# Retention followed by a multiplicative FFN: start-up orders, unswapped heads in first chunks, and two row products moved by half a step

## The chip, the cores and the metric

The kernel runs on one core of a Trainium2 chip. The metric is the device time of one execution in microseconds. Five executions of the kernel before gave 188.74, 189.39, 189.68, 190.88 and 192.08 us; the median, 189.68 us, is the time that the prediction refers to. One further execution was profiled.

The engines are called PE (TensorE, matrix products), PEld (its weight loads), DVE (VectorE), ACT (ScalarE), POOL (GpSimd) and SP (SyncE, which here issues nearly all DMAs). Matrix products write to PSUM banks, which DVE and ACT empty. Every engine works through its own instructions in the order in which the program gives them, and engines wait for each other by semaphores.

## The reference

There are 4 batches, 8 heads, 768 positions and a head size of 64. Per head a 64 x 64 state decays by a factor and takes up one outer product per position; its product with the query is the output. All heads of a position, 512 numbers, then pass a feed-forward block of width 1024 without biases:

```python
gamma = 1.0 - 2.0 ** (-5.0 - np.arange(H, dtype=np.float32))
for t in range(S):
    state = gamma[None, :, None, None] * state + np.einsum('bhd,bhe->bhde', k[:, :, t], v[:, :, t])
    y[:, :, t] = scale * np.einsum('bhd,bhde->bhe', q[:, :, t], state)
# x = y with the heads side by side, 3072 rows of 512
h = (x @ w1) * (x @ w2) @ w3
out = h @ w_out
```

## The kernel before

**Tiling.** The recurrence is done by chunks of C = 128 positions, in two halves s of L = 64. One step m treats one chunk of two batches (index e): there are NCH = 6 chunks to a pair of batches and two pairs, so NSTEP = 12, and steps 0 and 6 are first chunks, with no state behind them. The 8 heads are NP = 4 pairs p with r = 0, 1. Decays are split into factors per row: v is multiplied by VS when it is cast to 16 bits, the outputs by YS when they leave PSUM, the state by GS from chunk to chunk.

**The parts of a step.** `k_transposes`/`k_dma` and `q_transposes`/`q_dma` bring kT and qT. `scores(m)` (L367) makes 32 products of 64 x 64 into psA, and its `am_back(r)` (L374, DVE) masks them into `am`. `intra(m)` (L395) multiplies `am` by v into two banks psY (s = 0, 1). `kv(m)` (L415) makes the outer products psK of each half; `kv_back(0)` (L432 in a first chunk, L434 otherwise, DVE) and `kv_back(1)` (L429 on DVE, then L430 on POOL, which multiplies by GS) turn them into the states `t`. `inter(m)` (L460) adds the product of queries and states to psY. `outputs_back(m, s)` (L474, DVE) multiplies psY by YS into `XT[m]`, the input of the feed-forward block. These products use quarters of the 128 x 128 array: 64 x 64 with row group and column group chosen by the halves of the operands.

**Swapped heads.** In psY, half s = 1 has the two heads of a pair swapped between partitions 0 to 63 and 64 to 127: `side(s, r)` is `half(r ^ s)`. `outputs_back` puts them back, so for s = 1 it takes two DVE instructions on 64 partitions, each from one half of the partitions to the other. For s = 0 it is one on 128.

**The feed-forward block** works on transposed data. w3 and w_out are multiplied first, at the start: w3 is loaded, cast by ACT (L208), transposed by PE (L235, L244), copied by DVE (L227) and multiplied by w_out (L256, L269) to W3O. Then, per step, `a_unit(f)` and `b_unit(f)` (L494) make a 128-row block f of x @ w1 and x @ w2, ACT copies the first out of PSUM (`pa`, L503), and DVE multiplies the two into HT (L509). `o_unit(e)` (L519) multiplies the eight blocks of HT by W3O for one batch, ACT scales the result (L523) and a DMA stores it. These are called the row products here: `ab(f)` is a pair of them, 8 matmuls of 256 columns; an `o_unit` is 8 of 512.

**PSUM.** The pool `ps_f` has four banks. psF, psO and, from step 4 on, psK take them as they become free: a bank that `kv` fills is free again when its `kv_back` has read it. psY has banks Y0 and Y1, psA banks X0 and X1.

**Order.** The order of every engine is the order of the program, which is written by hand (`manual_schedule`). Loads go out on SP in the order of the calls; 22 staging buffers hold them, and the program's first lines issue all loads up to chunk 4. From line 539 to 668 stand steps 0 and 1 and the beginning of step 2, with `busy` and `keep_busy` calls that multiply zeros on PE. Then come `step2()` and `step(3)` to `step(12)`. From step 5 on a step has this order on PE: `intra(m-1)`, `kv(m)`, `scores(m)`, `inter(m-1)`, the two `o_unit`s of chunk m-2, and the eight `ab` of chunk m-1. On DVE it has the three instructions of `outputs_back(m-1)`, the two of `kv_back`, the two of `am_back`, and eight products L509. The last line of the loop over f in `step` (L743 to L744) puts `ab(4)` to `ab(7)` of chunk m-1 at the end of step m.

**Places that the change touches:** `output_decays` (L185 to L192), called at L554; `side` (L381); `back` in `kv` (L422 to L435); `inter` (L460); `outputs_back` (L468 to L478); the start-up from L584 to L658; and `step`.

Of the kernel before, what the change touches and what calls it, by code (L numbers as in the profile page):

```python
# [9 lines left out]
FP = mybir.dt.float32  # L10
HP = mybir.dt.float16
AF = mybir.ActivationFunctionType
MULT = mybir.AluOpType.mult
# [5 lines left out]
def kernel(  # L19
# [11 lines left out]
    nc = tc.nc  # L31
# [27 lines left out]
    def half(x):  # L59
        return slice(x * L, (x + 1) * L)  # L60
# [91 lines left out]
    if_i = const.tile([128, 2, L], mybir.dt.int32, name="if_i")  # L152
    nc.gpsimd.iota(if_i[:, :, :], pattern=[[L, 2], [1, 2], [2, 32]], base=1, channel_multiplier=0)
    LGH = const.tile([128, H], FP, name="LGH")
    LGP = const.tile([128, 2, H], FP, name="LGP")
    for h in range(H):
        nc.gpsimd.memset(LGH[:, h : h + 1], -math.log(gam[h]))
    for h in range(H):
        for s in range(2):
            u = h // 2 * 2  # L160
            nc.gpsimd.memset(LGP[half((h + s) % 2), s, u : u + 2], math.log(gam[h]))


    keep = const.tile([128, L], FP, name="keep")
# [6 lines left out]
        )  # L171

    VS = const.tile([128, H], FP, name="VS")
    YS = const.tile([128, 2, H, L], FP, name="YS")
    GS = const.tile([128, NP, 128], FP, name="GS")
    vs_x = const.tile([128, H], FP, name="vs_x")
    nc.vector.tensor_tensor(vs_x[:, :], ip_i[:, :], LGH[:, :], MULT)
    if_f = const.tile([128, 2, L], FP, name="if_f")
# [1 line left out]
    nc.scalar.activation(VS[:, :], vs_x[:, :], AF.Exp)  # L180
    for h in range(H):
        p, r = h // 2, (h % 2) * 64
        nc.gpsimd.memset(GS[r : r + 64, p, :], gam[h] ** C)

    def output_decays():  # L185
        for s in range(2):
            x = att.tile([128, H, L], FP, tag="s32", name="s32")
            nc.vector.tensor_tensor(
                x[:, :, :], if_f[:, s, :].unsqueeze(1).broadcast_to((128, H, L)),
                LGP[:, s, :].unsqueeze(2).broadcast_to((128, H, L)), MULT,  # L190
            )
            nc.scalar.activation(YS[:, s, :, :], x[:, :, :], AF.Exp)  # L192

    mark_t = const.tile([1, 1], HP, name="mark")
    XT = {}
# [184 lines left out]

    def side(s, r):
        return half(r ^ s)

    def intra(m):
        am, v16 = AMs[m], v16s[m]
        psYs[m] = ps = [bank(f"Y{s}", [128, NP * 2, L], FP, "psY") for s in range(2)]
        last = None
        for e in range(2):  # L390
            for p in range(NP):
                for s in range(2):
                    for r in range(2):
                        c0 = p * 128 + r * 64
                        last = nc.tensor.matmul(  # L395
                            ps[s][side(s, r), p * 2 + e, :], lhsT=v16[half(s), e, c0 : c0 + 64],
                            rhs=am[half(s), r, p * 2 + e, :], start=(e == 0 and p == 0),
                            stop=(m % NCH == 0 and s == 0 and e == 1 and p == NP - 1),
                        )
        return last  # L400

    def kv(m, psf=False):
        k16, v16 = k16s[m], v16s[m]
        c = m % NCH
        n = 2 if c < NCH - 1 else 1
        if psf:
            ps = [ps_f.tile([128, NP * 2, L], FP, tag="psF", name="psK") for s in range(n)]
        else:
            ps = [bank(f"X{s}", [128, NP * 2, L], FP, "psK") for s in range(n)]
        for e in range(2):  # L410
            for p in range(NP):
                for s in range(len(ps)):
                    for r in range(2):
                        c0 = p * 128 + r * 64
                        nc.tensor.matmul(  # L415
                            ps[s][half(r), p * 2 + e, :], lhsT=k16[half(s), e, c0 : c0 + 64],
                            rhs=v16[half(s), e, c0 : c0 + 64], start=True, stop=True,
                        )
        if c == 0:
            Ts[m, 0] = None  # L420

        def back(s, eng=nc.gpsimd):  # L422
            if s >= len(ps):
                return
            t16 = att.tile([128, NP * 2 * L], HP, tag="t16", name="t16", bufs=4)
            kvs = ps[s][:, :, :].rearrange("p u x -> p (u x)")
            if s == 1:
                s32 = att.tile([128, NP * 2 * L], FP, tag="s32", name="s32")
                nc.vector.tensor_tensor(s32[:, :], kvs, Ts[m, 1][:, :], ADD)  # L429
                eng.tensor_tensor(t16[:, :], s32[:, :], GS[:, :, :].rearrange("p a x -> p (a x)"), MULT)  # L430
            elif Ts[m, 0] is None:
                nc.vector.tensor_copy(t16[:, :], kvs)  # L432
            else:
                nc.vector.tensor_tensor(t16[:, :], kvs, Ts[m, 0][:, :], ADD)  # L434
            Ts[(m, 1) if s == 0 else (m + 1, 0)] = t16  # L435

        return back
# [14 lines left out]
    def inter(m, behind=None):  # L452
        ps = psYs[m]
        t = [Ts[m, s] for s in range(2)]
        for e in range(2):
            for p in range(NP):
                u = p * 2 + e
                for r in range(2):
                    for s in (1,) if t[0] is None else (0, 1):
                        mm = nc.tensor.matmul(  # L460
                            ps[s][side(s, r), u, :], lhsT=t[s][half(r), u * L : (u + 1) * L],
                            rhs=queries(m, e, p, s, r), start=False, stop=(e == 1 and p == NP - 1),
                        )
                        if behind is not None:
                            wait_for(mm, behind)
                            behind = None

    def outputs_back(m, s):  # L468
        if m not in XT:
            XT[m] = xpool.tile([128, NP * 2, 2, L], HP, tag="xt", name="xt")  # L470
        order = "p u (t i) -> p u t i"
        for to in (slice(0, 128),) if s == 0 else (half(0), half(1)):
            fr = to if s == 0 else half(1 - to.start // L)
            nc.vector.tensor_tensor(  # L474
                XT[m][to, :, s, :].rearrange("p u (i t) -> p u t i", t=2),
                psYs[m][s][fr, :, :].rearrange(order, t=2),
                YS[fr, s, :, :].rearrange(order, t=2), MULT,
            )  # L478

    class Ffn:  # L480
# [207 lines left out]
    def step(m):  # L688

        kv_backs = []  # L690

        def keys():
            if 3 < m < NSTEP:
                kv_backs.append(kv(m, True))

        if m > 4:
            last = intra(m - 1)
            last = ended(last)
            keys()
            if m < NSTEP:  # L700
                am_back = scores(m)
            inter(m - 1, last)
        else:
            inter(m - 1)
            keys()
            am_back = scores(m)
        outputs_back(m - 1, 0)
        outputs_back(m - 1, 1)
        if m >= NSTEP:
            return  # L710
        for kv_back in kv_backs:
# [24 lines left out]
        ffn[m - 1].ab(2)  # L736
        ffn[m - 1].ab(3)
        if m == 3:
            kv_back(1)
        if m % 2 == 0:  # L740
            q_cast(m + 2, nc.gpsimd)
            q_cast(m + 3, nc.gpsimd)
        for f in range(4, 8):  # L743
            ffn[m - 1].ab(f)  # L744

    step2()
    for m in range(3, NSTEP):
        step(m)
# [38 lines left out]
```

## Time and profile before

| | us |
|---|---|
| median of five executions | 189.68 |
| profiled execution, device time | 190.95 |
| its span, first to last instruction | 189.24 |
| PE busy | 176.6 (93%) |
| PE weight loads busy | 125.0 (66%) |
| DVE busy | 107.9 (57%) |
| ACT busy | 87.1 (46%) |
| POOL busy | 55.7 (29%) |

The DMA queues moved 40.25 MB, 213 GB/s over the span. The profiled execution was one of the longer ones, 1.27 us over the median; durations are taken from it, and times are counted from its span's start. In lists of groups "line engine op out<-in" names the kernel's line, the engine, and the tiles. In the list of waits stand the engine and line that waited, whom it waited for, the total, how often, and the longest. "Issue" is time in which an engine waited for nothing that the profile shows. In the answer by stretches each engine has busy time and, in brackets, its number of instructions; behind them stand PE's granted clock (1.00 is full speed), the busy share of the DMA engines and GB/s.

PE's busy time by stretch: 7.61 us in the first 10 us, 8.64 from 10 to 20, 9.73 from 20 to 30, 6.96 from 30 to 40, 9.32 from 60 to 70, 8.71 from 130 to 140, and 9.9 to 10.0 in the others up to 170.

### The profile page before, as it was taken

What the parts mean: (1) busy time and instruction counts of PE and PEld (TensorE: products, weight loads), DVE (VectorE), ACT (ScalarE), POOL (GpSimd) and SP (SyncE); (2) the same over time, 40 slices, a digit from 0 to 9 for tenths busy, and PEclk for the clock granted to TensorE, in tenths of its full rate; (3) what the DMA queues carried; (4) which work ended last, traced back from release to release, by engine and by line L of the source; (5) the groups of instructions that cost most, each with busy time, mean ns of one, the idle gap of its engine ahead of it and who ended that gap; (6) DMA issues with size and microseconds to landing.
All of it is one profiled execution on the core that took longest, in us unless ns stands there. A gap on an engine that the chain in (4) does not pass through costs nothing.

```text
span 189.2 us, 6256 instructions
## 1 busy us (share of the span) xinstructions
PE 176.6 (93%) x2655; PEld 125.0 (66%) x2655; DVE 107.9 (57%) x199; ACT 87.1 (46%) x170; POOL 55.7 (29%) x93
## 2 busy tenths in 40 slices
PE   7797998589999899999999999999979999999993
PEld 2353565258877578587785877858658688684872
DVE  1227447736166945956748577485674774845330
ACT  3477844445575354342644416444154353332432
POOL 7200234606741642172400826008251060000000
PEclk9999999979999999999999999999999999999999
DMA  5999999999899999999999999999969960200203
GB/s 192 376 386 400 276 205 262 399 406 255 180 231 244 195 214 194 242 243 267 218 182 239 238 258 205 177 230 246 262 152 206 210 173 0 77 37 3 111 3 111
DMA packets 87339, 40.25 MB, mean 213 GB/s; under 512 B 67728, under 2 KB 82320, under 8 KB 87312
## 3 DMA queue, kind: packets, MB, share of 16 engines
q1 hardware_dynamic: 86880, 39.33, 89.0%
q8 instruction: 21, 0.34, 0.8%
q10 hardware_dynamic: 432, 0.52, 0.8%
q14 instruction: 6, 0.05, 0.1%
HBM read 29.36 MB, written 6.29 MB: 188 GB/s over the span
## 4 chain that ended last, share of the span: by engine, by line
PE 79%; DVE 6%; DMA 5%; ACT 4%; issue 2%; SPq 2%; ACTq 0%; DVEq 0%
PE psF L494 37%; PE psO L519 21%; DMA stg<-in_moe_w_dram 5%; PE psF L605 4%; PE psW L269 3%; PE psY L395 2%; PE psA L367 2%; DVE xt L474 2%; PE psY L460 2%; SPq L63 2%; PE psG L494 2%; ACT w3h L208 2%; PE psK L415 1%; DVE am L374 1%; PE psTq L314 1%
## 5 line engine op out<-in xcount | busy, mean ns | idle before, releaser
L494 PE MATMUL psF<-xt,w 128*128 128x256 f16 x672 | 75.9, 273 | 0.0
L494 PEld LDWEIGHTS <-w 128*128 128x128 f16 x704 | 68.4, 98 | 10.2
L509 DVE TENSOR_TENSOR ht<-pa,psF 128x256 f16<-128x256 f32 x88 | 36.6, 419 | 36.6 <-PE psF L494 27.9
L503 ACT COPY pa<-psF 128x256 f32<-128x256 f32 x80 | 29.7, 371 | 35.3 <-PE psF L494 35.3
L519 PE MATMUL psO<-w3o,ht 128*128 128x512 f16 (+2 forms) x200 | 43.9, 371 | 1.3 <-DVE xt L474 1.3
L519 PEld LDWEIGHTS <-ht 128*128 128x128 f16 x200 | 18.5, 98 | 21.1 <-issue 1.6
L474 DVE TENSOR_TENSOR xt<-psY,YS 64x512 f16<-64x512 f32 (+1 forms) x36 | 26.2, 727 | 7.5 <-PE psY L460 7.1
L523 ACT ACTIVATE osb<-psO 128x512 f32<-128x512 f32 (+2 forms) x25 | 14.5, 580 | 33.3 <-PE psO L519 30.4
L430 POOL TENSOR_TENSOR t<-s,GS 128x512 f16<-128x512 f32 x10 | 12.7, 1273 | 55.4 <-DVE s L429 55.4
L302 POOL TENSOR_TENSOR v<-stg,VS 128x512 f16<-128x512 f32 x23 | 23.6, 1043 | 10.6 <-DMA stg<-in_v_dram 8.6
L281 POOL CAST q<-stg 128x1024 f16<-128x1024 f32 x9 | 9.3, 1038 | 26.3 <-DMA stg<-in_q_dram 26.3
L374 DVE TENSOR_TENSOR am<-psA,keep 128x512 f16<-128x512 f32 x24 | 15.4, 681 | 2.8 <-PE psA L367 2.7
L227 DVE COPY w3t<-psW 128x1024 f16<-128x1024 f16 x8 | 5.5, 692 | 13.4 <-PE psW L235 10.5
L295 ACT CAST k<-stg 128x1024 f16<-128x1024 f32 (+1 forms) x12 | 10.8, 899 | 1.7 <-DMA stg<-in_k_dram 1.7
L208 ACT CAST w3h<-stg 128x1024 f16<-128x1024 f32 x8 | 8.1, 1042 | 5.5 <-DMA stg<-in_moe_w_dram 5.5
L605 PE MATMUL psF<-xt,w 128*128 128x256 f16 x64 | 9.3, 302 | 0.1
L395 PE MATMUL psY<-am,v 64*64 64x64 f16 x384 | 6.2, 196 | 2.9 <-DVE xt L474 1.3
L395 PEld LDWEIGHTS <-v 64*64 64x64 f16 x384 | 4.4, 108 | 6.2 <-issue 5.8
L434 DVE TENSOR_TENSOR t<-psK,t 128x512 f16<-128x512 f32 x10 | 6.9, 690 | 2.6 <-PE psK L415 2.2
L537 PE MATMUL psZ<-zeros 128*128 128x512 f16 x16 | 6.9, 586 | 1.3 <-DVE zeros L144 1.3
L269 PE MATMUL psW<-wo,w3t 128*128 128x512 f16 x32 | 8.1, 380 | 0.0
L256 PE MATMUL psW<-wo,w3t 128*128 128x512 f16 x32 | 8.0, 384 | 0.0
(65 smaller groups left out, 128.0 us busy)
## 6 DMA issues: line engine op xcount, KB each, us to landing
stg<-in_moe_w_dram SPq DMA_DIRECT2D x16, 512.0 KB, 9.4
stg<-in_q_dram SPq DMA_DIRECT2D x12, 512.0 KB, 6.4
stg<-in_k_dram SPq DMA_DIRECT2D x24, 256.0 KB, 5.6
stg<-in_v_dram SPq DMA_DIRECT2D x24, 256.0 KB, 5.7
out_dram<-osb SPq DMA_DIRECT2D x22, 256.0 KB, 3.4
stg<-in_moe_w_out_dram SPq DMA_DIRECT2D x4, 512.0 KB, 7.8
out_dram<-osb ACTq DMA_DIRECT2D x1, 256.0 KB, 2.1
out_dram<-osb ACTq DMA_DIRECT2D x1, 160.0 KB, 1.8
```

Of the source, the lines that this page charges most:

```text
L269: nc.tensor.matmul(ps[:, :], lhsT=t[:, g * 128 : (g + 1) * 128], rhs=WO[g // 2][:, g % 2, :], start=(g == 0), stop=(g == 7),)
L302: eng.tensor_tensor(v16[:, e, :].rearrange("j (h d) -> j h d", d=D), v32[:, e, :].rearrange("j (h d) -> j h d", d=D), VS[:, :].unsqueeze(2 ...
L374: nc.vector.tensor_tensor(am[:, r, :, :], ps[r][:, :, :], keep[:, :].unsqueeze(1).broadcast_to((128, NP * 2, L)), MULT,)
L395: last = nc.tensor.matmul(ps[s][side(s, r), p * 2 + e, :], lhsT=v16[half(s), e, c0 : c0 + 64], rhs=am[half(s), r, p * 2 + e, :], start=(e ...
L430: eng.tensor_tensor(t16[:, :], s32[:, :], GS[:, :, :].rearrange("p a x -> p (a x)"), MULT)
L474: nc.vector.tensor_tensor(XT[m][to, :, s, :].rearrange("p u (i t) -> p u t i", t=2), psYs[m][s][fr, :, :].rearrange(order, t=2), YS[fr, s, ...
L494: nc.tensor.matmul(ps[:, :], lhsT=W[d][:, f * 128 : (f + 1) * 128], rhs=self.x(d), start=(d == 0), stop=(d == 3),)
L503: nc.scalar.copy(self.pa[f][:, :], ps[:, :])
L509: nc.vector.tensor_tensor(self.HT[:, f, :], self.pa.pop(f)[:, :], ps[:, :], MULT)
L519: nc.tensor.matmul(psO[:, :], lhsT=self.HT[:, f, e * 128 : (e + 1) * 128], rhs=W3O[f][:, cs], start=(f == 0), stop=(f == 7),)
L523: nc.scalar.activation(osb[:, cs], psO[:, :], AF.Copy, scale=final_scale)
L605: nc.tensor.matmul(ps[f // 2][:, f % 2, :], lhsT=W[d][:, f * 128 : (f + 1) * 128], rhs=f0.x(d), start=(d == 0 and f % 2 == 0), stop=(d == ...
```

## The change

There are seven edits.

1. YS holds one factor per pair of heads and position in place of one per (pair, batch): three variants, (s = 0), (s = 1, heads in place) and (s = 1, heads swapped). `output_decays` makes them in three DVE products of 128 x 256 and one Exp of 768 columns, and is called behind the first cast of w3 instead of behind the last cast of w_out. `outputs_back` reads YS with a stride of zero over the two batches.
2. GS shrinks to one number per pair and partition; POOL's product L430 reads it with a stride of zero.
3. In first chunks (steps 0 and 6) the heads of half s = 1 are not swapped, and `outputs_back(m, 1)` is one DVE instruction there.
4. In first chunks the copy of psK to `t` (L432) goes from DVE to ACT.
5. In step 0 `inter(0)` is called behind `outputs_back(0, 0)`, `v_cast(1)` and `kv_back(1)` of chunk 0, and `outputs_back(0, 1)` right behind it, ahead of `scores(1)` and its `am_back`s. PE's own order stays as it was.
6. In step 1 POOL casts W2[0] and W2[1] ahead of the state's product with GS, which moves behind `q_cast(2)`; its DVE sum stays between `by_rows(W1, ps, 1)` and `by_rows(W1, ps, 2)`.
7. In step 8 `ab(6)` and `ab(7)` of chunk 7 fall out; step 9, the tenth, has them behind `am_back` and ahead of `o_unit(0)` of chunk 7.

```diff
-    LGP = const.tile([128, 2, H], FP, name="LGP")
+    LGP = const.tile([128, 2, NP], FP, name="LGP")
...
-            u = h // 2 * 2
-            nc.gpsimd.memset(LGP[half((h + s) % 2), s, u : u + 2], math.log(gam[h]))
+            nc.gpsimd.memset(LGP[half((h + s) % 2), s, h // 2 : h // 2 + 1], math.log(gam[h]))
...
-    YS = const.tile([128, 2, H, L], FP, name="YS")
-    GS = const.tile([128, NP, 128], FP, name="GS")
+    YS = const.tile([128, 3, NP, L], FP, name="YS")
+    GS = const.tile([128, NP], FP, name="GS")
...
     def output_decays():
-        for s in range(2):
-            x = att.tile([128, H, L], FP, tag="s32", name="s32")
+        x = xpool.tile([128, 3, NP, L], FP, tag="xt", name="ys_x")
+        for n, (s, swap) in enumerate(((0, 0), (1, 0), (1, 1))):
             nc.vector.tensor_tensor(
-                x[:, :, :], if_f[:, s, :].unsqueeze(1).broadcast_to((128, H, L)),
-                LGP[:, s, :].unsqueeze(2).broadcast_to((128, H, L)), MULT,
+                x[:, n, :, :], if_f[:, s, :].unsqueeze(1).broadcast_to((128, NP, L)),
+                LGP[:, swap, :].unsqueeze(2).broadcast_to((128, NP, L)), MULT,
             )
-            nc.scalar.activation(YS[:, s, :, :], x[:, :, :], AF.Exp)
+        nc.scalar.activation(
+            YS[:, :, :, :].rearrange("p n a x -> p (n a x)"), x[:, :, :, :].rearrange("p n a x -> p (n a x)"), AF.Exp
+        )
...
-    def side(s, r):
-        return half(r ^ s)
+    def side(m, s, r):
+        return half(r if m % NCH == 0 else r ^ s)
...
-        def back(s, eng=nc.gpsimd):
+        def back(s, eng=nc.gpsimd, later=False):
...
-                eng.tensor_tensor(t16[:, :], s32[:, :], GS[:, :, :].rearrange("p a x -> p (a x)"), MULT)
+                def decay():
+                    eng.tensor_tensor(
+                        t16[:, :].rearrange("p (a x) -> p a x", a=NP), s32[:, :].rearrange("p (a x) -> p a x", a=NP),
+                        GS[:, :].unsqueeze(2).broadcast_to((128, NP, 2 * L)), MULT,
+                    )
+
+                if later:
+                    Ts[m + 1, 0] = t16
+                    return decay
+                decay()
             elif Ts[m, 0] is None:
-                nc.vector.tensor_copy(t16[:, :], kvs)
+                nc.scalar.copy(t16[:, :], kvs)
...
-        order = "p u (t i) -> p u t i"
-        for to in (slice(0, 128),) if s == 0 else (half(0), half(1)):
-            fr = to if s == 0 else half(1 - to.start // L)
+        swap = s == 1 and m % NCH > 0
+        for to in (half(0), half(1)) if swap else (slice(0, 128),):
+            fr = half(1 - to.start // L) if swap else to
+            n = fr.stop - fr.start
             nc.vector.tensor_tensor(
-                XT[m][to, :, s, :].rearrange("p u (i t) -> p u t i", t=2),
-                psYs[m][s][fr, :, :].rearrange(order, t=2),
-                YS[fr, s, :, :].rearrange(order, t=2), MULT,
+                XT[m][to, :, s, :].rearrange("p (a e) (i t) -> p a e t i", e=2, t=2),
+                psYs[m][s][fr, :, :].rearrange("p (a e) (t i) -> p a e t i", e=2, t=2),
+                YS[fr, s + swap, :, :].unsqueeze(2).broadcast_to((n, NP, 2, L))
+                .rearrange("p a e (t i) -> p a e t i", t=2),
+                MULT,
             )
...
     cast_w3(("c", 0), w3c_st[0])
+    output_decays()
     busy(8)
...
     cast_wo(3)
-    output_decays()
     cast_w3(4, w3_st[4])
...
     w3o_back()
-    inter(0)
     outputs_back(0, 0)
     v_cast(1, (nc.gpsimd, nc.gpsimd))
     backs[1](1)
+    inter(0)
+    outputs_back(0, 1)
     nc.gpsimd.tensor_copy(W1[1][:, :], w1_st[1][:, :])
...
     am_back(0)
     am_back(1)
-    outputs_back(0, 1)
     ps = four_banks()
...
     by_rows(W1, ps, 1)
-    kv_back(1)
     nc.gpsimd.tensor_copy(W2[0][:, :], w2_st[0][:, :])
     nc.gpsimd.tensor_copy(W2[1][:, :], w2_st[1][:, :])
+    decay = kv_back(1, later=True)
     by_rows(W1, ps, 2)
...
     q_cast(2, nc.gpsimd)
+    decay()
     by_rows(W2, ps, 2)
...
         am_back(0)
         am_back(1)
+        for f in behind.pop(m - 2, ()):
+            ffn[m - 2].ab(f)
         ffn[m - 2].o_unit(0)
...
         for f in range(4, 8):
-            ffn[m - 1].ab(f)
-
+            if f not in behind.get(m - 1, ()):
+                ffn[m - 1].ab(f)
+    behind = {7: (6, 7)}
     step2()
```

More of the change, by code (lines that the diff above doesn't have):

```diff
@@ L182 @@
         p, r = h // 2, (h % 2) * 64
-        nc.gpsimd.memset(GS[r : r + 64, p, :], gam[h] ** C)
+        nc.gpsimd.memset(GS[r : r + 64, p : p + 1], gam[h] ** C)
     def output_decays():
-        for s in range(2):
-            x = att.tile([128, H, L], FP, tag="s32", name="s32")
+        x = xpool.tile([128, 3, NP, L], FP, tag="xt", name="ys_x")
+        for n, (s, swap) in enumerate(((0, 0), (1, 0), (1, 1))):
             nc.vector.tensor_tensor(
-                x[:, :, :], if_f[:, s, :].unsqueeze(1).broadcast_to((128, H, L)),
-                LGP[:, s, :].unsqueeze(2).broadcast_to((128, H, L)), MULT,
-            )
-            nc.scalar.activation(YS[:, s, :, :], x[:, :, :], AF.Exp)
+                x[:, n, :, :], if_f[:, s, :].unsqueeze(1).broadcast_to((128, NP, L)),
+                LGP[:, swap, :].unsqueeze(2).broadcast_to((128, NP, L)), MULT,
+            )
+        nc.scalar.activation(
+            YS[:, :, :, :].rearrange("p n a x -> p (n a x)"), x[:, :, :, :].rearrange("p n a x -> p (n a x)"), AF.Exp
+        )
     mark_t = const.tile([1, 1], HP, name="mark")
@@ L395, in intra @@
                         last = nc.tensor.matmul(
-                            ps[s][side(s, r), p * 2 + e, :], lhsT=v16[half(s), e, c0 : c0 + 64],
+                            ps[s][side(m, s, r), p * 2 + e, :], lhsT=v16[half(s), e, c0 : c0 + 64],
                             rhs=am[half(s), r, p * 2 + e, :], start=(e == 0 and p == 0),
@@ L460, in inter @@
                         mm = nc.tensor.matmul(
-                            ps[s][side(s, r), u, :], lhsT=t[s][half(r), u * L : (u + 1) * L],
+                            ps[s][side(m, s, r), u, :], lhsT=t[s][half(r), u * L : (u + 1) * L],
                             rhs=queries(m, e, p, s, r), start=False, stop=(e == 1 and p == NP - 1),
```

## The prediction

> **What bounds the kernel now.** I read the chain that ended last first, then the waits of TensorE (PE), then timelines of every engine from 15 to 67 us and from 118 to 142 us, then busy time by stretches.
>
> The page's fourth part gives the chain's shares:
>
> ```profile
> PE 79%; DVE 6%; DMA 5%; ACT 4%; issue 2%; SPq 2%; ACTq 0%; DVEq 0%
> ```
>
> Behind 67 us nearly all of the chain is PE. A change there pays only where it closes a hole in PE's row. In front, the chain goes over loads, casts and VectorE (DVE). PE's waits, longest first, show the holes:
>
> ```profile
> PE psY L395 <- DVE xt L474: 1.3, 1, 1.3
> PE psO L519 <- DVE xt L474: 1.3, 1, 1.3
> ...
> PE psY L395 <- issue: 1.2, 1, 1.2
> ...
> PE psA L367 <- issue: 0.4, 1, 0.4
> ```
>
> The first and the third lie next to each other in the chain (start, length, what):
>
> ```profile
> 35.52 0.73 DVE xt L474
> 36.25 0.01 issue
> 36.26 0.73 DVE xt L474
> 36.99 0.04 issue
> 37.03 0.38 PE psY L395 x24
> 37.41 1.15 issue
> 38.57 0.25 PE psY L395 x6
> ```
>
> PE waits until the first chunk's two xt products are done, works for 0.38 us, and stands again in the middle of a matmul group, waiting for nothing that the profile names. The second wait is misnamed: `xt` had started at 135.40 and o_unit doesn't read it. I counted the matmuls ahead of each unexplained hole (the third number in brackets):
>
> ```profile
> 0.00:37.42 37.42, 31.51 (x351) 16.17 (x351) 18.07 (x30) 21.43 (x27) 12.10 (x51) 1.00 1.01 311
> 0.00:63.20 63.20, 55.77 (x735) 34.66 (x735) 31.04 (x55) 35.21 (x51) 21.06 (x61) 0.97 1.01 291
> 0.00:137.50 137.50, 129.11 (x2014) 89.49 (x2015) 80.84 (x147) 67.06 (x122) 49.10 (x87) 0.99 1.10 256
> ```
>
> 351, 735 and 2014 lie 384 and 1279 apart: 3 x 128 and, but for one, 10 x 128. With its weight load a matmul is two instructions, so the holes sit at the edges of blocks of 256 PE instructions. The page's DMA part agrees: queue q8, "instruction", brought 0.34 MB in 21 packets, 16 KB each, against 5310 matmuls and weight loads. In the trace's DMA records the packets in front of the holes ran at 36.24 to 37.19, 61.17 to 62.38 and 135.35 to 136.67; PE went on 1.4 to 1.6 us later. So a hole is a block of PE's program that came late. From PE's entry into the block ahead (matmuls 224, 608 and 1887, at 31.30, 59.29 and 134.06 us) to going on (38.57, 63.75, 138.23) it took 7.27, 4.46 and 4.17 us. Blocks full of 64x64 matmuls are run through faster than that.
>
> A last view, busy time by stretch (span, PE busy, ..., granted clock third from the end):
>
> ```profile
> 33.04:36.45 3.41, 2.48 (x41) 1.07 (x42) 2.90 (x6) 2.16 (x4) 2.82 (x3) 1.00 1.01 400
> 36.45:39.87 3.42, 1.69 (x68) 1.26 (x68) 1.22 (x2) 1.04 (x1) 0.44 (x1) 1.00 1.01 408
> 39.87:43.28 3.41, 3.41 (x47) 2.30 (x45) 1.67 (x4) 1.04 (x1) 0.00 (x0) 0.50 1.05 385
> 135.44:138.86 3.42, 2.13 (x10) 0.87 (x9) 3.33 (x5) 0.22 (x1) 1.01 (x1) 1.00 1.15 196
> ```
>
> After a stretch with PE busy for 1.69 us of 3.42 the clock was 0.50 for 3.41 us, which costs 3.41/2 = 1.7 us. After 2.48 and 2.13 us it stayed at 1.00.
>
> **The change, part by part.** (a) *YS early.* In before, DVE makes two `s` products at 16.02 (1.28 us) and ScalarE (ACT) two Exp at 16.74 (1.23 us), ahead of the cast of w3 rows 4 at 17.88, whose data landed at 16.2. Moved to the start, three products of 128x256 (under 0.64 us each, the 128x512 row) fall into DVE's idle 4.77 us before 7.06, and the Exp of 768 columns (0.62 x 1.5 = 0.93) into ACT's 2.12 us before 8.05: free. The casts then follow the landings (16.2, 17.5, 18.8, 20.1), PE reaches w3_mm(6) about 0.8 us sooner, and meets the next limit: k's second half lands at 26.37, its ACT cast (0.62) ends at 27.02, so the key transposes can end at 27.44 instead of 28.06. The first chunk's am and intra come 0.4 to 0.65 us sooner; I take 0.65.
>
> (b) *First chunk.* DVE loses the copy of psK (0.69, L432) and one of the two half products (0.73), and the other stands ahead of am(1). The copy goes to ACT (0.60 by the 128x512 row of L208) at about 31.2, when kv(0) ends; ACT's kT copies wait until 32.06, so it is covered, with 0.2 us to spare. DVE: xt half 0 at 31.0 to 31.73, s at 31.87 to 32.54, then inter(0) is ready and xt half 1 runs to 33.3; scores(1) end at 33.7, am(1) at 35.0. intra(1) can start at 35.05 instead of 37.03: 2.0 us sooner.
>
> (c) *What is late next* is matmul 352, 24 matmuls into intra(1), reached at 35.4. Its block is asked for 0.65 us sooner (30.65). With the 7.27 us of the same place it goes on at 37.92; with the 4.46 us of the next place it would be there at 35.1, before PE. The lower gain is 0 (transfer paced by the loads in front), the upper 38.57 - 35.4 = 3.2. The load is the same at that place, so I take 7.27: **gain 0.65 us**, not 2.0. PE's idle time there becomes 0.4 + 2.5 us, against 1.5 + 1.15 now, so I leave the halved clock in place: 0 (end of the range: 1.7 gained).
>
> (d) *GpSimd's (POOL) order and the late decay.* POOL idled 7.55 us before 44.44, waiting for `s`. Now the W2 casts go ahead; from 39 to 58 us PE has no wait for them in before, so this gives 0, and covers PE being sooner: W2[0] and W2[1] land at 41.16 and 42.44, casts done by 43.5, needed at about 46. The decay moves behind q_cast(2) (48.05 to 49.3); `t` is read by the next chunk's DVE add at 60.72. q_cast(3) and k_cast(2) behind it on POOL end by 51, needed at 53. GS with a stride of zero: L302 reads VS that way at 1.04 us, the decay has 1.27; either is hidden. The block at matmul 736 shifts with its entry: 0; if it came at its old time, the 0.65 would be lost.
>
> (e) *Sixth-chunk start.* DVE saves 0.73 + 0.69 us and ACT gets 0.60 in its 2.4 us wait for psO; PE has no hole from 75 to 135 us: 0. The new patterns of xt keep 512 elements: 0.73, as now. If they cost some tenths more, PE's cover is the free banks behind o_unit.
>
> (f) *Tenth step.* 16 matmuls (1.75 us) move behind inter(8) and in front of o_unit of chunk 7. The block in front of matmul 2015 then lasts 1.5 us longer (1.75 less the 24 intra matmuls that fall out), more than the 1.29 us that it was late: that hole closes. But HT 6 and 7 now come on DVE behind these:
>
> ```profile
> 135.40 2.20 DVE L474 TENSOR_TENSOR xt<-psY,YS 128x512 f16<-128x512 f32 x3 [0.81 <-PE psY L460]
> 137.64 0.69 DVE L434 TENSOR_TENSOR t<-psK,t 128x512 f16<-128x512 f32 x1
> 138.36 0.69 DVE L429 TENSOR_TENSOR s<-psK,t 128x512 f32<-128x512 f32 x1
> 138.97 1.28 DVE L374 TENSOR_TENSOR am<-psA,keep 128x512 f16<-128x512 f32 x2
> ```
>
> From the first to the last it is 140.25 - 135.40 = 4.85 us. inter(8) now ends 1.75 us sooner, so DVE starts at 133.65 and am ends at 138.5; the two ht products (0.42 each, 0.40 apart) end at 138.9 and 139.25. PE has run the 16 matmuls and six of o_unit(0) by then (the kv banks, held until L434 and L429 end at 136.6 and 137.3, already stop it for about 1 us), waits, ends o_unit(0) at 139.5 and o_unit(1) (8 x 0.2225) at 141.3. In before that end was 140.33: **loss 0.97 us**. The 1.29 us hole is exchanged for 2.4 us of waiting for DVE and banks. In an execution whose block is not late the loss is 2.3.
>
> **Sum** on the profiled execution: 190.95 - 0.65 + 0.97 = 191.27, of which the span is 189.24 + 0.32 and 1.7 lies around it. That execution is 1.27 above the median, so I carry the difference: 189.68 + 0.32 = 190.0.
>
> The Trainium skill speaks to two terms. "Runtime: NRT & Kernel Launch", section "Instruction fetch mechanics", says that each engine streams its program in 16 KiB blocks of 256 instructions while it runs the one before, and that crossing an edge is mostly hidden; the block size agrees with the counts, the hiding doesn't (1.15, 0.40 and 1.29 us of holes). Were it hidden, (c) would give 2 us and (f) cost 2.3. "TensorE: Matmul & The Clock Gate", Part 1, says that the clock is halved after an idle window of about 3.4 us; here it was halved with no wait over 1.5 us. By the page's rule the tenth step couldn't lose its clock and the slower rival below would go.
>
> **Rivals.** *Faster: the block is there in time.* At the 4.46 us of the second place, intra(1) runs through, 3.2 us are gained, the stretch stays busy and the clock whole (1.7 more): 189.68 - 3.2 - 1.7 + 0.97 = 185.8. Two thirds of the wait gone and the clock kept gives about 187.5. For it: two of three places took 4.2 to 4.5. Against: the loads of w1 and w2 are at their densest there (400 GB/s). Chance 0.2, at 187.
>
> *Slower: the clock is halved in the tenth step.* Its waits of 0.45, 0.7, 0.95 and 0.2 us lie between 135.0 and 139.3; a 3.41 us stretch from 135.9 holds 1.56 us of work, under the 1.69 that lost the clock; one from 134.5 holds 2.2, over the 2.13 that kept it. Somewhere between it decides, and how the stretches fall is chance. Price 1.7: 191.7; if the block also wasn't late in most executions of before, 193.0. Chance 0.3.
>
> *The change doesn't do what it says:* the block edge slips to another instruction of step nine and PE waits for both. o_unit then ends no later than DVE lets it, so it is the forecast's time.
>
> **How the numbers follow.** The forecast 0.5 (own range 189.0 to 191.2), faster rival 0.2, slower 0.3. The time is 190.0. To leave out no more than 2 in 10 the range runs from 187.0 to 192.3. 1% (1.9 us) is about what a measurement of this kernel can tell from no change: below 187.8 is most of the faster rival, 0.18; above 191.6 most of the slower one, 0.27; within, 0.55.
>
> **What would show it.** Right: first w3 row cast at 16.2; am(1) ends near 35.0; PE stands at matmul 352 until about 37.9; no "issue" hole in the tenth step's o_unit, but waits for DVE ht in it, and the step about 1 us longer than 13.25. Wrong: no hole at matmul 352, a clock of 1.00 from 40 to 43 us, or o_unit of chunk 7 starting with both ht products done.

## The result, and the profile after

The changed kernel takes 191.25 us (median of 44 executions, 189.28 to 194.83) against 189.71 us for the kernel before (median of 79). The ratio is 1.0056, with a 95% interval of 1.0038 to 1.0074: about 1.1 us slower. It is formed, like all ratios below, only from executions within 1.5% of the fastest of their kernel (29 of the 44), which leaves out most of those whose clock was halved for a while. The prediction was 190.0 us, 0.3 over before, with 0.55 on "within 1%".

The profiled execution took 192.93 us, 1.7 over its kernel's median, as before's 190.95 was 1.3 over. Its span is 190.87 us, 1.63 more than before. The time around the span has grown too, from 1.71 to 2.06 us, and that is so throughout: device time less span has a median of 1.71 to 1.77 us in every run of a kernel with the old start-up, and of 2.04 to 2.10 in every run with the new one. So about 0.3 of the 1.1 us lies ahead of the first instruction or behind the last. Which edit brings it is not shown.

PE's waits, with engine and line, whom it waited for, the total, how often and the longest, are now these:

```profile
PE psF L509 <- ACT osb L538: 2.2, 1, 2.2
...
PE psY L397 <- issue: 0.8, 1, 0.8
PE psO L534 <- DVE ht L524: 0.8, 1, 0.8
...
PE psF L509 <- ACT pa L518: 0.5, 1, 0.5
PE psO L534 <- DVE t L446: 0.4, 1, 0.4
```

The 1.3 us for the xt products are gone, the unexplained hole has shrunk from 1.2 to 0.8, and the tenth step's misnamed 1.3 us has given way to the last three lines. The first line is new, and it is the largest.

In the chain (start, length, what) the start-up now reads

```profile
33.67 1.28 DVE am L375 x2
34.95 0.04 issue
34.99 0.39 PE psY L397 x25
35.37 0.84 issue
36.21 0.25 PE psY L397 x6
...
59.35 6.24 DMA stg<-in_k_dram
```

In before, intra(1) started at 37.03 and went on after its hole at 38.57; now it starts at 34.99 and goes on at 36.21, 2.4 us sooner. By inter(2) PE is 3.05 us ahead (59.30 against 62.35). Then the chain leaves PE for a load: chunk 4's second half of k lands at 65.59. In before it landed at 65.21, so the load isn't sooner although PE is, and in before its cast, which followed other work of ACT, had no wait for it:

```profile
66.49 1.04 ACT L295 CAST k<-stg 128x1024 f16<-128x1024 f32 x1
```

The changed kernel's ACT timeline shows what hangs on it (start, length, engine, line, operation, in brackets the idle time ahead and whom it waited for):

```profile
65.99 1.04 ACT L296 CAST k<-stg 128x1024 f16<-128x1024 f32 x1 [2.26 <-DMA stg<-in_k_dram]
66.94 0.59 ACT L538 ACTIVATE osb<-psO 128x512 f32<-128x512 f32 x1
67.43 0.64 ACT L518 COPY pa<-psF 128x256 f32<-128x256 f32 x2
```

The cast of k waits 2.26 us for the load; the copies of pa stand behind it and hold PSUM banks, so PE stops at 65.35 until 67.58. And that stop has a second price (span, PE busy, ..., granted clock third from the end):

```profile
64.83:68.24 3.41, 1.19 (x25) 0.74 (x27) 0.42 (x1) 2.08 (x4) 1.66 (x2) 1.00 0.97 300
68.24:71.65 3.41, 3.41 (x77) 2.61 (x73) 1.54 (x4) 0.37 (x1) 0.39 (x1) 0.50 1.18 137
```

After a stretch with 1.19 us of work in 3.41 the clock was halved for 3.41 us, 1.7 us of work lost. In before the same had happened at 39.87 to 43.28. So both executions lost it once, at different places, and the eight `ab` of step 4 start at 80.12 against 79.83: of 3.05 us nothing is left.

The tenth step, in before PE at the late block, which the profile puts down to xt:

```profile
135.25 1.69 PE L519 MATMUL psO<-w3o,ht 128*128 128x512 f16 x7
138.23 2.10 PE L519 MATMUL psO<-w3o,ht 128*128 128x512 f16 x9 [1.29 <-DVE xt L474]
```

In the changed kernel DVE:

```profile
134.28 2.21 DVE L487 TENSOR_TENSOR xt<-psY,YS 128x512 f16<-128x512 f32 x3 [0.80 <-PE psY L472]
136.52 0.69 DVE L446 TENSOR_TENSOR t<-psK,t 128x512 f16<-128x512 f32 x1
137.25 0.69 DVE L431 TENSOR_TENSOR s<-psK,t 128x512 f32<-128x512 f32 x1
137.85 1.28 DVE L375 TENSOR_TENSOR am<-psA,keep 128x512 f16<-128x512 f32 x2
139.05 0.74 DVE L524 TENSOR_TENSOR ht<-pa,psF 128x256 f16<-128x256 f32 x2
```

and PE:

```profile
134.13 1.67 PE L509 MATMUL psF<-xt,w 128*128 128x256 f16 x12
136.26 0.60 PE L509 MATMUL psF<-xt,w 128*128 128x256 f16 x4 [0.46 <-ACT pa L518]
137.27 1.47 PE L534 MATMUL psO<-w3o,ht 128*128 128x512 f16 x6 [0.41 <-DVE t L446]
139.51 2.45 PE L534 MATMUL psO<-w3o,ht 128*128 128x512 f16 x10 [0.78 <-DVE ht L524]
```

PE runs the two moved row products, waits for ACT's copy, for a bank that `kv_back` still holds, and after six of o_unit's matmuls for HT 6, which DVE makes as the last of its list. The same 160 matmuls (`ab(6)` and `ab(7)` of chunk 7, the quarters of the tenth step, the two o_units of chunk 7; matmuls 1864 to 2023 of the trace in both kernels) take 8.92 us from the start of the first to that of the next `ab` (132.88 to 141.80), in before 8.01 (132.16 to 140.17). Behind them both kernels need 45.63 us to the start of their last matmul.

Two theories stood behind this. **A:** the front's gain is spent on the loads, so the front gives nothing, and the move costs about 1 us for DVE's order. **B:** the move pays for itself because the late block costs more in most executions than in the profiled one, and the loss is the front's. Ratios below are to runs of the kernel before on the same chip in the same session.

### The profile page after: what moved, and what is told of

The parts are those of the page before. It is cut to its first block, busy times and chain, and to the rows that moved or that the text cites. A ratio compares the mean times of both kernels' runs of the same rounds, so it can differ in the third digit from the quotient of the medians.

```text
span 190.9 us, 6255 instructions
## 1 busy us (share of the span) xinstructions
PE 177.6 (93%) x2655; PEld 125.2 (66%) x2655; DVE 105.0 (55%) x196; ACT 88.4 (46%) x171; POOL 52.9 (28%) x93
## 4 chain that ended last, share of the span: by engine, by line
PE 62%; DMA 19%; SPq 8%; DVE 4%; ACT 2%; issue 2%; ACTq 0%; DVEq 0%
PE psF L509 34%; PE psO L534 18%; DMA stg<-in_k_dram 9%; SPq L63 8%; DMA stg<-in_moe_w_out_dram 4%; DMA kT<-k 3%; DMA stg<-in_v_dram 2%; PE psF L621 2%; PE psY L397 2%; DVE am L375 2%; PE psY L472 2%; PE psA L368 2%; PE psK L417 1%; PE psG L509 1%; DVE xt L487 1%
## 5 line engine op out<-in xcount | busy, mean ns | idle before, releaser
L509 PEld LDWEIGHTS <-w 128*128 128x128 f16 x704 | 69.1, 99 | 13.9 <-issue 3.2
L487 DVE TENSOR_TENSOR xt<-psY,YS 64x512 f16<-64x512 f32 (+1 forms) x34 | 24.7, 728 | 7.7 <-PE psY L472 6.8
L434 POOL TENSOR_TENSOR t<-s,GS 128x512 f16<-128x512 f32 x10 | 10.4, 1039 | 46.5 <-DVE s L431 46.5
L257 PE MATMUL psW<-wo,w3t 128*128 128x512 f16 x32 | 8.5, 402 | 0.0
L270 PE MATMUL psW<-wo,w3t 128*128 128x512 f16 x32 | 8.1, 380 | 0.4 <-DVE w3t L228 0.4
```

The source lines that it names most:

```text
L487: nc.vector.tensor_tensor(XT[m][to, :, s, :].rearrange("p (a e) (i t) -> p a e t i", e=2, t=2), psYs[m][s][fr, :, :].rearrange("p (a e) (t ...
L509: nc.tensor.matmul(ps[:, :], lhsT=W[d][:, f * 128 : (f + 1) * 128], rhs=self.x(d), start=(d == 0), stop=(d == 3),)
```

## Experiments

**1. The front without the move.**

```diff
-    behind = {7: (6, 7)}
+    behind = {}
```

> The changed kernel without the move in the tenth step; all else as changed. Theory A (the front's gain is spent again on waiting for chunk 4's keys and on a halved clock, and the move costs what DVE's order makes it wait): about 1.1 us under the changed kernel, 190.1 us, 0 to 0.5 us over the kernel before; matmuls 2008 to 2015 show the unexplained hole of about 1.3 us again. Rival B (the move pays for itself because the late block costs more in most executions than in the profiled one, and the loss lies in front): no faster than the changed kernel, 191.3 us or more.

Measured: 1.0011 (0.9955 to 1.0066). The interval allows a loss or a gain of some tenths of a per cent, so as a time this only says that the front gives no gain near 3 us. The trace says more: the hole is back at the eighth matmul of o_unit (1.28 us), the 160 matmuls take 7.99 us, and the stop for the keys is there (1.90 us, until 67.91).

**2. The move alone, in the kernel before.**

```diff
+        for f in behind.pop(m - 2, ()):
+            ffn[m - 2].ab(f)
         ffn[m - 2].o_unit(0)
...
-            ffn[m - 1].ab(f)
+            if f not in behind.get(m - 1, ()):
+                ffn[m - 1].ab(f)
```

> The kernel before with only the move of the two row products in the tenth step. Theory A: 1.0 to 1.2 us slower than before, 190.8 us; no unexplained hole in that step, but waits for DVE and for PSUM banks of about 2.4 us. Rival B: not slower than before, 189.7 us or less. If the waits bring a halved clock, 1.7 us more, 192.5.

Measured: 1.0035 (0.9997 to 1.0073). In its trace the 160 matmuls take 9.01 us, 1.00 more than before, with waits of 0.46, 0.41 and 0.78 us for ACT, the bank and HT. In the trace the move costs 1 us, as A says; as a time it is 0.7 us, with an interval that just reaches no change. B's gain isn't there. The two halves, +0.35% and +0.11%, make up the change's +0.56% within their intervals.

This execution had the old front with a whole clock. Its eight `ab` of step 4 start at 77.65. In the first experiment, with the new front and a whole clock, they start at 78.90.

**3. The keys' cast behind the first `ab`s.**

```diff
+        late = m in (3, 4)
...
-            k_cast(m + 1, (nc.scalar,))
+            if not late:
+                k_cast(m + 1, (nc.scalar,))
...
         ffn[m - 2].o_unit(1)
+        if late:
+            for f in range(2):
+                ffn[m - 1].ab(f)
+            k_cast(m + 1, (nc.scalar,))
...
-        for f in range(2):
+        for f in () if late else range(2):
...
-    behind = {7: (6, 7)}
+    behind = {}
```

> As the first one, and in steps 3 and 4 the ACT cast of the next chunk's keys (with its transposing DMA) stands behind ab(0) and ab(1) and not between the two o_units. Theory A: the changed kernel stands still for 2.2 us behind 65.1 because ACT waits for chunk 4's keys (landing near 65.6) with the copies of pa queued behind, and then loses 1.7 us to a clock of 0.5. With the copies ahead, both go: 186.5 to 188 us, the first figure if no later load takes their place. Rival: the keys are not what bounds it but all loads together, so the wait comes back one step later: 189.5 to 190.1 us.

Measured: 1.0043 (0.9999 to 1.0086). The stop behind 65 us is gone, as A expected of ACT's order, but not the time. The rival was right that the wait comes back later (1.0043 is 190.5 us, a little over its 189.5 to 190.1). PE stops elsewhere, at scores(4) and later in step 5:

```profile
PE psA L368 <- DMA kT<-k: 1.3, 1, 1.3
...
PE psF L509 <- ACT osb L538: 1.1, 1, 1.1
```

The second is the same pattern one step on: at 90.14 ACT's cast of k had waited 1.87 us for its load. In these traces the order of ACT changed where PE stopped for the loads, not whether.

**4. Zeros in the wait.**

```diff
         ffn[m - 2].o_unit(1)
+        if m == 3:
+            busy(10, "X1")
...
-    behind = {7: (6, 7)}
+    behind = {}
```

> As the first one, with ten products of zeros (2.2 us of PE) put into step 3 behind the o_units, where PE would stand still. They add nothing to the result. If the idle time causes the halved clock, the clock stays at 1.00 behind 68 us and the run is up to 1.7 us under the first one (188.4 us); if the clock falls for another reason, or rarely, no difference (190.1 us); if the wait was not there in most executions, up to 2.2 us slower (192.3 us).

Measured: 1.0103 (1.0043 to 1.0163), slower. The profiled execution had no stop in step 3 and a clock of 1.00 throughout, but four of the six executions had a mean clock of 0.991, so the zeros didn't keep it. Where it fell in those isn't recorded. This doesn't settle what the zeros cost or save, and the rule for the clock stays open.

**5. Block edges moved by 24 matmuls** (one execution; timed in experiment 10):

```diff
-    busy(8)
+    psz = bank("Y0", [128, 512], FP, "psZ")
+    for _ in range(32):
+        nc.tensor.matmul(psz[:, 0:128], lhsT=Z[:, 0:128], rhs=Z[:, 0:128], start=True, stop=True)
```

> The kernel before; the first eight products of zeros (512 columns) are made as 32 of 128 columns: the same columns, 24 more matmuls on PE while it waits for the first cast. Theory A (the unexplained holes are edges of blocks of 256 PE instructions): they stay at matmuls 352, 736 and 2015 counted from the start, so they move to other work: 2015 into inter(8), 24 matmuls ahead of o_unit, and 352 to the first matmuls of intra(1), where it hides behind the wait for xt. Rival (the holes belong to the work: a transfer, a bank or a semaphore of o_unit): they stay at o_unit's eighth matmul and at the 25th of intra(1), now matmuls 2039 and 376.

One execution: 188.43 us. There is no hole at matmul 2015, 2039 or 736, and none at 376; the wait ahead of matmul 352, now the first of intra(1), is the 1.3 us for xt. So the holes weren't where the rival had them, but there was none at the new place either, and in experiment 2, without the 24 matmuls, there was none at 352 or 736: one execution doesn't decide here, experiment 10 does. PE stopped for 1.05 us in the next `ab`s behind the cast of chunk 10's keys, which landed at 137.29.

**6. HT ahead of xt, in the kernel before.** The two row products stand behind the quarters on PE as in the change, but are called ahead of `outputs_back`, so DVE makes HT 6 and 7 first:

```diff
             inter(m - 1, last)
+            for f in behind.pop(m - 2, ()):
+                ffn[m - 2].ab(f)
...
-            ffn[m - 1].ab(f)
+            if f not in behind.get(m - 1, ()):
+                ffn[m - 1].ab(f)
...
+    behind = {7: (6, 7)}
```

> The kernel before with the two row products behind the quarters of the tenth step, as in the change, but called ahead of outputs_back, so that DVE makes HT 6 and 7 before xt, kv and am. Theory A (the move loses because DVE has HT behind 4.85 us of other work): no wait of o_unit for DVE, no late block; o_unit(1) of chunk 7 ends 1.2 to 1.4 us sooner than in before, so 0.993 to 0.994 of before, 1.0 to 1.4 us faster. Rival (the move itself costs: banks or ACT's copies behind the quarters): at best as before, 0.998 or more.

Measured: 0.9985 (0.9945 to 1.0024). The waits for HT and banks are gone, so A is right on them, but in the profiled execution the block was late all the same: PE entered the block ahead at 131.45 and went on behind its edge at 137.48, 6.0 us later, where it had been 4.2 in before; 1.16 us of it PE stood. Expected were 0.993 to 0.994. How late a block is changes from execution to execution.

**7. One load less.**

```diff
-        load_q(m + 2) if m < 4 else None
+        if m == 2:
+            load_q(4)
+        if m == 3:
+            q_in[5] = q_in[4]
...
-    behind = {7: (6, 7)}
+    behind = {}
```

> The changed kernel without the move in the tenth step, and without the 512 KB load of the sixth q tile: its place is taken by the fifth, so the queries of one batch are wrong from there on; all instructions but that load stay. Theory A (up to about 90 us the stream of loads bounds the front, so what the front gains is given back): chunk 4's keys land some 2 us sooner, near 63.5, the stop of 1.9 to 2.2 us behind ab(1) in step 3 is gone or under 0.5 us, and the run is 1.5 to 2.2 us faster than the first experiment. Rival (ACT's order or the staging buffers, not the stream): landing and wait stay, no faster than the first experiment.

This kernel leaves out the sixth q tile, so its output is not the reference's from there on. Measured: 0.9890 (0.9850 to 0.9931), 2.1 us under before, against +0.2 for the first experiment on another chip: 2.3 us, where A expected 1.5 to 2.2. The two intervals leave about 1.3 us of doubt either way. The keys landed at 63.96 (65.94 in the first experiment), and ACT's timeline shows the wait for them halved:

```profile
64.04 1.04 ACT L299 CAST k<-stg 128x1024 f16<-128x1024 f32 x1 [1.17 <-DMA stg<-in_k_dram]
```

PE's stop there fell from 1.90 to 0.35 us, and the eight `ab` of step 4 start at 76.62, where they start at 78.90 in the first experiment. Single landings vary, though: in experiments 11 and 12, with all loads, the keys landed at 64.10 and 63.81. So it is the time of ten executions that carries this. Taking 512 KB out of the stream makes the whole kernel faster by about what 512 KB take at the 180 to 255 GB/s that before's page shows between 43 and 71 us (2.1 to 2.9 us), as expected if the stream of loads bounds the front.

**8. HT ahead of xt, in the changed kernel,** the edit of experiment 6 with the new front:

> The changed kernel with the two row products called ahead of outputs_back in the tenth step. Theory A: 2.0 to 2.4 us faster than the changed kernel, since DVE's wait (2.4 us) goes and the block isn't late: 0.993 to 0.997 of before, no better than the kernel before with the same edit, because the front's edits give nothing once the loads bound it. Rival (the front's edits keep some of their 3 us): faster than the kernel before with the same edit by 1 us or more.

Measured: 0.9927 (0.9892 to 0.9962). The 160 matmuls took 7.15 us and the block wasn't late. Beside experiment 6 (0.9985, same chip) it looks as if the front kept 1 us after all, which neither the first experiment nor the starts of step 4 show. So both were tried again with other pairs:

**9 to 12, on one chip.** The changed kernel itself; the kernel before with the edges moved (as in 5); the changed front without the move, with the edges moved; and experiment 8 once more.

> The changed kernel itself, beside the next three on one chip. Expected at 1.004 to 1.007 of before; the stretch from ab(6) of chunk 7 to its o_unit(1) (matmuls 1864 to 2023) 8.9 to 9.0 us, with no late block.

> The kernel before with the 24 more matmuls ahead, which move the block edges and leave all work where it was. If the late block of the tenth step is worth what it was in the profile, 1.0 to 1.4 us faster than before (0.993 to 0.995); if chunk 10's keys, which land near 138 us, take its place as in the single execution of this kernel (a stop of 1.05 us for them), 0.997 to 1.0.

> The changed front without the move, with the 24 more matmuls ahead. Theory A (the loads bound the front, its edits give nothing): within 0.5 us of the kernel before with the same 24 matmuls. Rival (the front's edits keep 1 us of their gain, as the eighth experiment beside the sixth seems to say): 1 us faster than that, 0.99 of before.

> The eighth experiment's kernel once more, beside the changed kernel on one chip: the two row products called ahead of outputs_back. Expected 1.6 to 2.4 us faster than the changed kernel and 0.991 to 0.996 of before, the tenth step's stretch 7.1 to 7.2 us; if that result was chance, within 0.5 us of the kernel before.

| | ratio to before (95%) | the 160 matmuls, us | `ab`s of step 4 start, us |
|---|---|---|---|
| changed kernel | 1.0050 (1.0014 to 1.0086) | 8.92 | 77.83 |
| before, edges moved | 0.9889 (0.9836 to 0.9942) | 7.26 | 77.37 |
| new front, no move, edges moved | 0.9989 (0.9949 to 1.0029) | 7.60 | 77.07 |
| new front, HT ahead of xt | 0.9946 (0.9910 to 0.9982) | 7.20 | 78.06 |

The last start includes a halved clock at 38.15 to 41.56; the other three had none ahead of it.

The changed kernel's loss and the stretch of 8.92 us came again, this time with a whole clock; the stop for chunk 4's keys was 1.40 us. With HT made ahead of xt the same move gains: the kernel is about 1.0% faster than the changed one, and the stretch 1.7 us shorter. The trace shows why: PE no longer waits for HT or banks, and only 0.21 us are left at the block's edge, where the profile names nothing:

```profile
133.86 1.67 PE L534 MATMUL psO<-w3o,ht 128*128 128x512 f16 x7
135.74 2.10 PE L534 MATMUL psO<-w3o,ht 128*128 128x512 f16 x9 [0.21 <-issue]
```

Moving nothing but the block edges in the kernel before gave 0.9889 in six executions, the lowest ratio of the kernels that do all the work, though its interval meets those of experiments 8 and 12, and lower than either expectation. (Experiment 5 was one execution of the same kernel: 188.43 us against a median of 189.67 for before on its chip.) Its trace lacks 2.3 us of the holes in before's: 1.15 at matmul 352 (now inside the wait for xt), 0.40 at 736, and 1.29 less 0.52 at 2015. That this is near the 2.1 measured proves little, since before's profiled execution was a long one that also lost 1.7 us to the clock, and in the traces of experiments 2 and 6, which have the old front without the 24 matmuls, the holes at 352 are 0 and 0.15 us and there is none at 736. Against experiment 2, whose clock was whole as well, the `ab`s of step 4 start only 0.28 us sooner; against before the 160 matmuls take 0.75 us less. So the traces account for about 1.0 of the 2.1 us, and the rest stays open. The PE timeline shows the late block where theory puts it:

```profile
132.82 0.33 PE L460 MATMUL psY<-qT,t 64*64 64x64 f16 x15
133.67 0.32 PE L460 MATMUL psY<-qT,t 64*64 64x64 f16 x17 [0.52 <-issue]
133.93 3.63 PE L519 MATMUL psO<-w3o,ht 128*128 128x512 f16 x16
```

The hole is in inter(8), and by the stretch's count

```profile
0.00:133.40 133.40, 124.52 (x2014) 89.18 (x2015) 78.72 (x144) 67.08 (x122) 49.09 (x87) 1.00 1.11 261
```

2014 matmuls lie ahead of it, exactly as in before, though the work there is 24 matmuls earlier. The trace of experiment 4 agrees: its ten products of zeros shift the work by ten, and a hole of 1.60 us lies in its inter(8), with 2014 matmuls ahead once more. The hole is tied to the count of instructions, and the instruction packet in front of it ran here from 130.94 to 132.15; PE went on 1.5 us later, as at before's holes. The hole is smaller (0.52 us) mainly because the block came sooner: from entering the block ahead to going on it took 3.65 us (130.02 to 133.67), in before 4.17, and PE ran through the block ahead in 3.13 us, in before in 2.88.

The new front with the same edges moved is 1% behind the old front (0.9989 against 0.9889), where A expected no difference and the rival a gain. About 0.3 us of this is the time around the span; no profile explains the rest: the two profiled spans are 186.06 and 186.45 us. The old front's figure rests on six executions. Nor do the 24 matmuls gain anything clear of noise with the new front (0.9989 against 1.0011 in experiment 1, on another chip). That the front gives nothing near its 3 us is shown; what it costs beyond the 0.3 us stays open.

## Why the prediction was right, point by point

- **(a), (b) the start-up's DVE and ACT path.** Right. am(1) was to end at 35.0 and ended at 34.95; intra(1) was to start at 35.05 and started at 34.99. The first w3 row cast came at 15.80 (predicted 16.2), chunk 0's am at 29.17, 0.58 us sooner (predicted 0.65).
- **(c) the block at matmul 352.** The mechanism was right, but the size was off: from its entry (30.72) PE went on after 5.5 us, not 7.27, so the gain at that place was 2.4 us and not 0.65. In the other traces in which PE stands there for the block it was 5.3 to 6.4 us, and in experiments 1, 2 and 11 the block was in time. A span taken from one execution was used as if it belonged to the place.
- **The clock in the start-up.** The forecast left before's halved clock in place; it stayed at 1.00 there and fell at 68 us instead, so the term of zero held, but by luck.
- **(d) is the step that failed.** It took W2 and the next chunk's casts as the last loads that matter and carried the front's gain on to the end. The trace of before shows k of chunk 4 landing at 65.21 and its cast on ACT at 66.49: the front could be at most about 1.3 us sooner there before that load became the bound. The forecast's 0.65 would have fitted into that; what the sum had no term for is that this landing doesn't move with the front and differs from execution to execution: 63.63 to 65.21 us in the five traces with the old front, 63.81 to 66.33 in the eight with the new one and all loads. Where the clock was whole up to there, the `ab`s of step 4 start at 77.37 to 77.65 with the old front (experiments 2, 5, 10) and at 77.07 to 78.90 with the new one (1, 8, 9, 11). Experiments 3 and 7 point to the loads as what takes the gain back. By luck the errors nearly cancel in the profiled execution: (c) too small by 1.7 us, (d) without the loads' 2.2 us. What was to be -0.65 came out as +0.2 (interval -0.9 to +1.3) in experiment 1.
- **(e)** Right: no wait of PE in step 7.
- **(f) the tenth step.** Right in mechanism and size: loss 0.97 predicted, 0.91 in the changed kernel's trace and 1.00 with the move alone. The waits were put at 0.45, 0.7, 0.95 and 0.2 us and measured 0.46, 0.41 and 0.78. Beside experiment 5, where the block wasn't late and the 160 matmuls took 6.56 us, the loss is 2.4, as the prediction has it for that case (2.3).
- **The rivals.** The faster one had its first half come true (the block was nearly in time, the clock whole) and still gave no gain, since the loads stood behind it. The slower one, a halved clock in the tenth step, showed in no trace with the move (clock 1.00 there in all three); where it fell in the other executions isn't recorded. Its yardstick, PE's work in 3.41 us, doesn't decide: 1.64 us kept the clock in experiment 3, 1.90 lost it in experiment 6 (last section).
- **The signs.** The holes and waits of the tenth step, am(1) and the loss came as named under "right"; PE stood at matmul 352, but until 36.21 and not 37.9. One of the signs of being wrong came true as well: a clock of 1.00 from 40 to 43 us.
- **The sum.** +0.32 us was forecast, +1.06 measured. Some 0.3 of the missing 0.7 is the time around the span, which the prediction carried over as 1.7 us without a reason and which measured about 2.05. That leaves +0.7 within the span, of which the move is 0.9 to 1.0; for the front there remain -0.2 to -0.3 in place of -0.65, which is within the noise of nothing. The forecast was near because its largest term, (f), was right and the front's errors were small or cancelled.

## What to carry to other kernels

When edits bring a start-up forward, look for the next load that somebody behind them waits for, and compare its landing with its use: the smallest slack on the way is the most that can be kept. When work is moved to fill a hole on one engine, follow its results too: here the row products filled PE's hole, but their consumers' inputs came last in DVE's list, and putting them first there turned a loss of 0.5% into a gain of 0.5%. Holes that nobody released, at a fixed distance counted in instructions, were edges of program blocks here, and a few instructions more at a place where the engine waits anyway can move them to other work: that gained about 1% with the old front, and nothing clear of noise with the new one. And a term that is carried over unchanged, as the time around the span was, belongs on the list of what to check.

## What the runs showed of the hardware that was not expected

- Where PE stood for a block of its program, it went on 3.3 to 6.0 us after entering the block ahead in the tenth step, and 5.3 to 7.3 us after it at matmul 352. The time differs between executions of the same program: in experiment 5 PE ran through the block ahead in 2.94 us without a stop, in experiment 10, the same kernel, it took 3.65 with one of 0.52. Twenty-four matmuls more at the start, with the same columns, made the kernel before 1.1% faster (0.9836 to 0.9942). The Trainium skill, "Runtime: NRT & Kernel Launch", section "Instruction fetch mechanics", has blocks of 256 instructions, which agrees with the counts, and says that crossing an edge is mostly hidden: in before's trace that is so at 17 of 20 edges, while the other three cost 0.40, 1.15 and 1.29 us; the longest in any trace is 1.77 us (experiment 3).
- The clock was halved for 3.41 us behind stretches of 3.41 us with 1.19 us of PE work (the changed kernel), 1.66 (experiment 12), 1.69 (before) and 1.90 (experiment 6); no single stop in them was over 2.23 us. It stayed at 1.00 behind such stretches, counted in steps of 3.41 us from the halvings at the trace's end, with 1.64 us (experiment 3), 1.80 (8), 1.81 (4 and 9) and 1.88 (1). So neither the time that PE is busy nor one long stop gives the rule, and it stays open.
- Leaving out one load of 512 KB made a kernel whose PE is busy for 92 to 94% of the span about 2 us faster (0.9850 to 0.9931 of before).
- Device time holds 1.7 us around the span with the old start-up and 2.05 with the new one, in every run; nothing in the traces names what it is.
